# GpSimd instead of VectorE scales the queries, and three of SP's transfers change place, in a fused attention and FFN kernel

## The chip, the cores and the metric

The kernel runs on one core of a Trainium2 chip. The metric is the time of one execution on the device, in microseconds (us). Several runs of a kernel give a median. One more execution is recorded by the hardware profiler, and all rows below come from it.

The engines are called as the profile calls them: PE is TensorE (the matrix unit; PEld is its weight load), DVE is VectorE, ACT is ScalarE, POOL is GpSimd, and SP is SyncE, which here issues all transfers in one order of its own (SPq in the rows).

## What is computed

Windowed attention over q, k, v of shape 4 x 8 x 768 x 64 (batch, heads, positions, head width), then a feed-forward net (FFN) with a rational function in its middle, over the 3072 tokens:

```python
scores = q @ k.T / sqrt(D) - slope[h] * dist          # dist: distance, or n_local for a global key
keep   = (key < n_global) | ((0 <= rel) & (rel < n_local))    # n_global = 8, n_local = 96
a      = softmax(where(keep, scores, -1e9))
x      = (a @ v), heads side by side                  # 3072 x 512
h      = x @ w_in                                     # 3072 x 2048
P      = a0 + a1*h + a2*h**2 + a3*h**3
Q      = 1 + |b0|*|h| + |b1|*h**2
out    = (P / (Q + 1e-6)) @ w_out                     # 3072 x 512
```

## The kernel before, in words

**Tiles and units.** A unit u is two heads on one tile of 128 positions. There are 96 units, four to a tile and eight to a chunk of 256 tokens, so 12 chunks. A chunk has eight FFN parts f, each 256 of the 2048 inner columns; there are 96 parts too. From unit 24 on, units are handled as pairs (u even, u and u+1: four heads).

**Steps.** The main loop of `windowed` counts steps t. Step t issues the work of several stages, each for its own unit or part: FFN part k = t - 12 goes through its first product (`st_ffn1`, L340), the part before it finishes its function, and the part two back goes through its second product (`st_ffn2`, L434). The attention of the pairs runs ahead in the same loop: even steps start a pair's loads, odd steps start its scores. The second product of part f thus stands two steps behind its first on PE, and in between lie, for one part: ACT's three operations on h (L365 to L367), the sum of two of them (`st_sum`, L379, on POOL for nearly all parts), ACT's logarithm and exponential (L390, L391), three operations of DVE (L395 to L397), ACT's rounded copy g (L405) and its remainder (`st_low`, L408, on POOL for nearly all parts). PE needs both copies for the second product.

**A pair of units.** For pair u the stages are: `st_load` (L179, L180: q and k into a tile nat, two buffers); `st_split`, which scales q by a factor per head (L497, DVE) and transposes the scaled q and the k in blocks of 32 (L500, DVE) into sp; `st_scatter` (L508, four transfers from sp to a block of DRAM, zq); `st_gather` (L515, back from zq into qk); `st_score` (L590, PE); the maximum, the exponentials, the sum and the norm (L625 on DVE, L634 on ACT, L639 and L641 on DVE, L647 on POOL); `st_pT` (L667, DVE's transpose into T); `st_spread` (L678, four transfers from T to z in DRAM); `st_pTE` (L694, back as pT, two buffers); and `st_pv` (L713, PE: four units at once, the product with the values). The values come as vt (`load_v`, L187: the pair's own tile of positions) and vp (`load_vp`, L198 and L199: the tile before it, six and two buffers). A chunk's output goes from the accumulator into a tile o (L467, ACT in the paired stage) and out by `st_send` (L474).

**What sets the order.** The first part of the program (the list LEAD, up to about unit 30) has the order of every engine written out by hand. After it, PE and SP issue in the order in which the loop writes the stages; each stage has a priority within its step (the table PRI). ACT, DVE and POOL get their order from a scheduler, which may place an instruction ahead of its step if it holds it to be ready. On the chip each engine then runs its instructions strictly in that order, and an instruction that waits holds up all behind it. SP does the same with its transfers.

**Where the loop puts the edits.** In the loop, `on(name, u, kinds)` writes the stages `kinds` of unit u at step t: before the change, odd steps write sr (gather) for t+1, tw (spread) for t-3 and zw (scatter) for t+3; even steps write P (pT) for t-4, L (q and k) for t+6, V (vt) for t and vp for t-4; the split for t+4 is written ahead of the FFN's function, and T for t-2 near the end of the even step. The last part of a chunk writes O and D (the output's copy and its transfer) in its own, odd, step.

Of the kernel before, what the change touches and what calls it, by code (L numbers as in the profile page):

```python
# [2 lines left out]

# [6 lines left out]
F32 = mybir.dt.float32  # L10
# [4 lines left out]
ALU = mybir.AluOpType  # L15
PSUM = bass.MemoryType.PSUM

P = 128
# [16 lines left out]
FIXED = 30  # L35
# [8 lines left out]
SUM_V = ((0, 1), (1, 1), (2, 1), (0, 2), (1, 2), (2, 2), (1, 3), (0, 5), (0, 6), (1, 7))  # L44
# [98 lines left out]
def tile_kernel(ctx: ExitStack, tc: tile.TileContext, q, k, v, n_global, n_local,  # L143
                w_in, w_out, ca, cb, out):
    nc = tc.nc
# [6 lines left out]
    NCH = B * S // TOK  # L152
# [30 lines left out]
    def load_v(u):  # L183
        c, t, p, b, i = unit(u)
        hs = slice(2 * p, 2 * p + 4)
        vts[u // 2] = vt = pl.ldp.tile([P, 4, D], F32, tag="vt", name=f"vt{u}", bufs=6)
        nc.sync.dma_start(out=vt, in_=v[b, hs, i * P:(i + 1) * P, :].rearrange("h s d -> s h d"))  # L187


# [2 lines left out]
    def load_vp(u):  # L192
        c, t, p, b, i = unit(u)
        if u < PAIRS or i == 0:
            return
        hs = slice(2 * p, 2 * p + 4)
        vps[u // 2] = vp = pl.ldp.tile([P, 4, D], F32, tag="vp", name=f"vp{u}", bufs=2)
        nc.sync.dma_start(out=vp[0:P - KB], in_=v[b, hs, (i - 1) * P + KB:i * P, :].rearrange("h s d -> s h d"))  # L198
        nc.sync.dma_start(out=vp[P - KB:], in_=v[b, hs, 0:KB, :].rearrange("h s d -> s h d"))  # L199

# [142 lines left out]


    BOTH = slice(0, 2)

    def side(f, early, late=False):
        if pl.split:
            return nc.gpsimd
        return nc.vector if f == NU - 2 or late or divmod(f, FPC) in early else nc.gpsimd  # L350
# [25 lines left out]

    def st_sum(f, ys=BOTH):
        a, s = (ew[f][n][:, ys] for n in "as")
        side(f, SUM_V).tensor_tensor(out=a, in0=a, in1=s, op=ALU.add)  # L379

    def st_ew2(f, ys=BOTH):
        st_poly(f, ys)
# [22 lines left out]
        nc.scalar.copy(out=gs[f][:, 0, ys], in_=ew[f]["u"][:, ys])  # L405

    def st_low(f, ys=BOTH):
        side(f, G_V, f == NU - 1 and ys == 1).tensor_tensor(out=gs[f][:, 1, ys], in0=ew[f]["u"][:, ys], in1=gs[f][:, 0, ys], op=ALU.subtract)  # L408

    def st_split_g(f, ys=BOTH):  # L410
        if not plain(f):
# [80 lines left out]
    def st_split(u):  # L492
        c, t, p, b, i = unit(u)
        if u < PAIRS or u % 2:
            return
        n = nat[u // 2]
        nc.vector.tensor_tensor(out=n[:, 0], in0=n[:, 0], in1=qsc[:, 2 * p:2 * p + 4].unsqueeze(2).broadcast_to([P, 4, D]),  # L497
                                op=ALU.mult)
        sp[u] = s = pl.att.tile([P, 4, 4, KB], F32, tag="rawq", name=f"sp{u}", bufs=2)
        nc.vector.transpose(out=s.rearrange("p b z t -> p z b t"),  # L500
                            in_=n.rearrange("p z (y x) (c d) -> p (z y) (x c) d", x=2, d=KB))
# [254 lines left out]
    def windowed():  # L756
# [26 lines left out]
        def part(kind, *args):  # L783
            if (kind, *args) not in done:
                done.add((kind, *args))
                parts[kind](*args)
# [20 lines left out]
        lead = [(c, j) for z in range(2) for c in range(2) for j in range(z * HALF, HALF if z == 0 else FPC)]  # L807
        steps = [c * FPC + j for c, j in lead] + list(range(2 * FPC, NU))

        for t in range(NU + LAG + F2):  # L810
            k = t - LAG
            u0 = t - 3 - run_of(t - 4)

            def on(name, u, *kinds):
                if 0 <= u < NU:
                    tc.cur_priority = base + 1000 * t + PRI[name]
                    for kind in kinds:
                        part(kind, u)

            def ffn(name, k, kind, *args):  # L820
                if 0 <= k < NU:
                    tc.cur_priority = base + 1000 * t + PRI[name]
                    part(kind, steps[k], *args)

            def ffn2(name, k, x):
                if 0 <= k < NU:
                    c, j = divmod(steps[k], FPC)
                    tc.cur_priority = base + 1000 * t + PRI[name]
                    part("f2", steps[k], x)
                    if j == cut_of(c) - 1 and j < FPC - 1:  # L830
                        part("H", c, x)
                    if j == FPC - 1:
                        part("O", c, x)
                        part("D", c, x)

            if k == NU - 2:
                with tc.manual_schedule(engines={mybir.EngineType.Activation, mybir.EngineType.DVE, mybir.EngineType.Pool, mybir.EngineType.SP}):
# [2 lines left out]
                        token(word, True)  # L840
                break
            fixed = t >= FIXED
            if t % 2:
                on("gather", t + 1, "sr")
                on("load", t - 3, "tw")
                on("load", t + 3, "zw")
            else:
                on("load", t - 4, "P")
                on("load", t + 6, "L")
                on("load", t, "V")  # L850
                on("load", t - 4, "vp")
            if t < FIXED:
                on("score", t - 2, "s", "kg", "t")
                on("soft", t - 2, "x", "r")
# [7 lines left out]
            if t < FIXED:  # L862
# [2 lines left out]
                    on("pv", u0, "o", "vg")  # L865
                    on("x", u0, "y", "z")
                on("qkE", t, "qE", "kG")
            if t % 2 == 0:
                on("split", t + 4, "sp")
                on("split", t - 2, "kG")  # L870
            ffn("ew3", k - 1, "e3")
            if t < FIXED:
                on("norm", t - 2, "n")
# [5 lines left out]
                ffn("ew4", k - 1, "gl")  # L879
            ffn("ew2", k, "e2")  # L880
            ffn("ew2", k, "eq")
            if fixed:
                on("score", t - 1, "t")
                for u in (t - 1, t) if t % 2 else (t - 1,):
                    on("soft", u, "x", "r")
                    on("norm", u, "n")
            on("pT", t - 2, "T")
            if t < FIXED:
                on("pT", t - 3, "P")
            ffn2("ffn2a", k - F2, 0)  # L890
# [167 lines left out]
```

## Time and profile before

| what | value |
|---|---|
| median of 3 runs | 748.62 us (747.9 to 755.06) |
| the profiled execution | 753.98 us, of which 752.2 us is the span from first to last instruction |
| mean granted clock of PE | 0.967 of full speed |
| busy share of the span | PE 92%, DVE 74%, ACT 71%, POOL 46% |

PE has the highest share, but the average hides the stages: the first 230 us load and convert the weights and run the written-out order, the stretch from 230 to 690 us is the paired stage at its steady pace, and the rest is the FFN's tail. A row of a timeline gives the start, the length, the engine, the line, the operation and its tiles; in square brackets stands how long the engine had been idle before it and which instruction ended that. "x4" are four instructions merged into a row. [...]

### The profile page before, as it was taken

To read this page: it belongs to the slowest core of one execution; us is meant where nothing else is said; L and a number is where in the kernel's file an instruction comes from. 1 tells how busy PE (TensorE), PEld (TensorE's weight loads), DVE (VectorE), ACT (ScalarE), POOL (GpSimd) and SP (SyncE) were. 2 spreads that over 40 slices of the span, in tenths; PEclk is the share of its full clock that TensorE was granted. 3 is DMA by queue.
4 is the path that set the end of the run, shared out by engine and by line. 5 is a ranking of instruction groups with operands and counts; after the bars stand their busy time and mean duration, and the time that the engine had idled before them with its cause. 6 is when DMAs were issued, how large, how long until landed. Compare 5 with 4: busy or idle time off the path is not lost.

```text
span 752.2 us, 17016 instructions
## 1 busy us (share of the span) xinstructions
PE 689.7 (92%) x6167; PEld 587.1 (78%) x6167; DVE 558.2 (74%) x1355; ACT 531.4 (71%) x1174; POOL 343.8 (46%) x451
## 2 busy tenths in 40 slices
PE   5799998999489998989997998998996989999996
PEld 4576777677478887878886887887885978989995
DVE  5899998989657767778667777767775767665665
ACT  6899996967257757757775766766765757766764
POOL 2354558464225435445434444454443534544441
PEclk9999999999798999999999999999998999999999
DMA  8874536031673483483364483383264483250001
GB/s 201 239 219 145 151 120 207 13 99 38 164 189 103 118 215 103 115 217 78 112 178 108 117 217 97 111 223 76 87 161 104 109 214 102 83 164 2 28 1 34
DMA packets 161212, 95.20 MB, mean 127 GB/s; under 512 B 100064, under 2 KB 141152, under 8 KB 161120
## 3 DMA queue, kind: packets, MB, share of 16 engines
q1 hardware_dynamic: 161120, 94.02, 46.9%
q8 instruction: 51, 0.84, 0.5%
q14 instruction: 41, 0.34, 0.1%
HBM read 66.39 MB, written 27.59 MB: 125 GB/s over the span
## 4 chain that ended last, share of the span: by engine, by line
PE 54%; ACT 13%; DMA 9%; DVE 8%; SPq 8%; issue 4%; POOL 4%; DVEq 0%; POOLq 0%
PE h L340 22%; PE acc L434 22%; PE o L713 4%; ACT pr L634 3%; PE s L590 3%; DMA vp<-in_v_dram 2%; DMA z<-T 2%; DMA nat<-in_k_dram 2%; ACT fu L365 2%; SPq L678 1%; ACT fa L366 1%; POOL g L408 1%; DVE q L396 1%; POOL pr L647 1%; POOL fa L379 1%
## 5 line engine op out<-in xcount | busy, mean ns | idle before, releaser
L379 POOL TENSOR_TENSOR fa<-fa,fs 128x512 f32<-128x512 f32 (+1 forms) x86 | 110.0, 1279 | 173.7 <-ACT fs L367 164.6
L647 POOL TENSOR_SCALAR pr<-pr,stats 128x160 f32<-128x160 f32 (+2 forms) x170 | 68.5, 420 | 163.1 <-DVE stats L641 118.7
L434 PE MATMUL acc<-h,g 128*128 128x512 f32 x336 | 117.2, 411 | 16.1 <-POOL g L408 11.6
L390 ACT ACTIVATE fs<-fa,coef 128x512 f32<-128x512 f32 (+1 forms) x97 | 69.9, 720 | 77.6 <-POOL fa L379 74.7
L434 PE MATMUL acc<-wout_h,g 128*128 128x512 f32 x352 | 118.9, 398 | 3.2 <-ACT g L405 2.0
L408 POOL TENSOR_TENSOR g<-fu,g 128x512 fp32r<-128x512 f32 x84 | 108.6, 1293 | 19.9 <-ACT g L405 10.8
L395 DVE SCALAR_TENSOR_TENSOR fu<-fu,coef,q 128x512 f32<-128x512 f32 (+1 forms) x97 | 71.7, 739 | 45.4 <-ACT q L391 43.7
L365 ACT ACTIVATE fu<-h,coef 128x512 f32<-128x512 f32 x94 | 72.9, 776 | 45.7 <-PE h L340 45.0
L634 ACT ACTIVATE pr<-pr,stats 128x160 f32<-128x160 f32 (+2 forms) x192 | 82.3, 431 | 32.2 <-DVE stats L625 32.0
L340 PE MATMUL h<-xh,win_h 128*128 128x256 f32 x352 | 102.9, 292 | 0.1
L340 PE MATMUL h<-xh,h 128*128 128x256 f32 x352 | 101.7, 289 | 0.0
L340 PE MATMUL h<-xl,win_h 128*128 128x256 f32 x352 | 99.5, 283 | 0.5 <-DVE xl L752 0.5
L340 PE MATMUL h<-xl,h 128*128 128x256 f32 x352 | 98.8, 281 | 0.0
L374 DVE TENSOR_TENSOR fu<-fu,h 128x512 f32<-128x512 f32 (+1 forms) x97 | 65.3, 673 | 35.2 <-ACT fs L367 35.2
L434 PEld LDWEIGHTS acc<-h,g 128*128 128x128 f32 x336 | 66.2, 199 | 31.6 <-POOL g L408 13.9
L434 PEld LDWEIGHTS acc<-wout_h,g 128*128 128x128 f32 x352 | 66.9, 191 | 16.7 <-POOL g L408 2.2
L405 ACT CAST g<-fu 128x512 fp32r<-128x512 f32 (+1 forms) x88 | 54.5, 619 | 33.5 <-DVE fu L397 33.3
L375 DVE SCALAR_TENSOR_TENSOR fu<-fu,coef,h 128x512 f32<-128x512 f32 (+1 forms) x97 | 71.2, 734 | 2.5
L396 DVE SCALAR_TENSOR_TENSOR q<-fa,coef,q 128x512 f32<-128x512 f32 (+1 forms) x97 | 72.2, 744 | 0.0
L340 PEld LDWEIGHTS h<-xh,win_h 128*128 128x128 f32 x352 | 67.3, 191 | 4.8 <-issue 2.3
L340 PEld LDWEIGHTS h<-xh,h 128*128 128x128 f32 x352 | 66.6, 189 | 4.3 <-issue 2.8
L340 PEld LDWEIGHTS h<-xl,win_h 128*128 128x128 f32 x352 | 67.4, 192 | 2.1 <-DVE xl L752 0.7
(262 smaller groups left out, 1709.7 us busy)
## 6 DMA issues: line engine op xcount, KB each, us to landing
pT<-z SPq DMA_DIRECT2D x30, 512.0 KB, 3.9
z<-T SPq DMA_DIRECT2D x120, 80.0 KB, 2.2
zq<-sp SPq DMA_DIRECT2D x144, 64.0 KB, 1.8
qk<-zq SPq DMA_DIRECT2D x36, 256.0 KB, 3.2
r<-in_moe_w_in_dram SPq DMA_DIRECT2D x16, 512.0 KB, 5.2
r<-in_moe_w_out_dram SPq DMA_DIRECT2D x16, 512.0 KB, 3.8
nat<-in_q_dram SPq DMA_DIRECT2D x48, 128.0 KB, 4.2
nat<-in_k_dram SPq DMA_DIRECT2D x48, 128.0 KB, 4.2
```

The source lines that it names most:

```text
L340: nc.tensor.matmul(out=h_of(f, y), lhsT=w[:, fs], rhs=x[:, ct, :], start=(n == 0), stop=(n == 3 * NCT - 1))
L365: nc.scalar.activation(out=u, in_=h, func=AF.Identity, scale=a3, bias=a2)
L374: nc.vector.tensor_tensor(out=u, in0=u, in1=h, op=ALU.mult)
L375: nc.vector.scalar_tensor_tensor(out=u, in0=u, scalar=a1, in1=h, op0=ALU.add, op1=ALU.mult)
L379: side(f, SUM_V).tensor_tensor(out=a, in0=a, in1=s, op=ALU.add)
L390: nc.scalar.activation(out=s, in_=a, func=AF.Ln, bias=q1)
L395: nc.vector.scalar_tensor_tensor(out=u, in0=u, scalar=a0, in1=r, op0=ALU.add, op1=ALU.mult)
L396: nc.vector.scalar_tensor_tensor(out=r, in0=a, scalar=q1, in1=r, op0=ALU.add, op1=ALU.mult)
L408: side(f, G_V, f == NU - 1 and ys == 1).tensor_tensor(out=gs[f][:, 1, ys], in0=ew[f]["u"][:, ys], in1=gs[f][:, 0, ys], op=ALU.subtract)
L434: nc.tensor.matmul(out=acc, lhsT=gs[f][:, z, y, ts], rhs=w, start=(start and n == 0), stop=(stop and n == 2))
L634: nc.scalar.activation(out=d, in_=d, func=AF.Exp, scale=-1.0, bias=st[:, x:x + 1], accum_out=st[:, 2 + 2 * x:3 + 2 * x])
L647: (nc.vector if u < NORMS else nc.gpsimd).tensor_scalar(out=d, in0=d, scalar1=st[:, 6 + x:7 + x], scalar2=0.0, op0=ALU.mult, op1=ALU.add)
```

## The change

Four edits. The scaling of q moves from DVE to POOL. In the paired stage, the split (scaling, transpose and a small copy) is written later in its step, behind the FFN's sums, and its instructions are issued only behind the last of POOL's FFN operations (sum or remainder) recorded up to there. vp is loaded two steps earlier, and shares eight buffers with vt. In SP's order the spread of T follows directly on T, ahead of the gather; pT is written at the end of the odd step; and a chunk's output goes out one step later, behind the spread.

```diff
     def load_v(u):
-        vts[u // 2] = vt = pl.ldp.tile([P, 4, D], F32, tag="vt", name=f"vt{u}", bufs=6)
+        vts[u // 2] = vt = pl.ldp.tile([P, 4, D], F32, tag="vt", name=f"vt{u}", bufs=8)
...
     def load_vp(u):
-        vps[u // 2] = vp = pl.ldp.tile([P, 4, D], F32, tag="vp", name=f"vp{u}", bufs=2)
+        vps[u // 2] = vp = pl.ldp.tile([P, 4, D], F32, tag="vt", name=f"vp{u}", bufs=8)
...
+    paced = {}
+
+    def pace(i):
+        paced[i.ins.engine] = i.ins
+
+    def behind(engine):
+        return tc.issue_after(paced[engine]) if paced.get("on") else nullcontext()
...
     def st_sum(f, ys=BOTH):
-        side(f, SUM_V).tensor_tensor(out=a, in0=a, in1=s, op=ALU.add)
+        pace(side(f, SUM_V).tensor_tensor(out=a, in0=a, in1=s, op=ALU.add))
...
     def st_low(f, ys=BOTH):
-        side(f, G_V, f == NU - 1 and ys == 1).tensor_tensor(out=gs[f][:, 1, ys], in0=ew[f]["u"][:, ys], in1=gs[f][:, 0, ys], op=ALU.subtract)
+        pace(side(f, G_V, f == NU - 1 and ys == 1).tensor_tensor(out=gs[f][:, 1, ys], in0=ew[f]["u"][:, ys], in1=gs[f][:, 0, ys],
+                                                                 op=ALU.subtract))
...
     def st_split(u):
-        nc.vector.tensor_tensor(out=n[:, 0], in0=n[:, 0], in1=qsc[:, 2 * p:2 * p + 4].unsqueeze(2).broadcast_to([P, 4, D]),
+        nc.gpsimd.tensor_tensor(out=n[:, 0], in0=n[:, 0], in1=qsc[:, 2 * p:2 * p + 4].unsqueeze(2).broadcast_to([P, 4, D]),
                                 op=ALU.mult)
...
                     if j == FPC - 1:
                         part("O", c, x)
-                        part("D", c, x)
+                        if c < NCH - 1:
+                            late.append((c, x))
+                        else:
+                            part("D", c, x)
...
             fixed = t >= FIXED
+            paced["on"] = t >= FIXED
             if t % 2:
                 on("gather", t + 1, "sr")
-                on("load", t - 3, "tw")
                 on("load", t + 3, "zw")
+                on("load", t - 3, "P")
             else:
-                on("load", t - 4, "P")
                 on("load", t + 6, "L")
                 on("load", t, "V")
-                on("load", t - 4, "vp")
+                on("load", t - 2, "vp")
...
-            if t % 2 == 0:
-                on("split", t + 4, "sp")
-                on("split", t - 2, "kG")
             ffn("ew3", k - 1, "e3")
...
             ffn("ew2", k, "eq")
+            if t % 2 == 0:
+                with behind(mybir.EngineType.Pool):
+                    on("split", t + 4, "sp")
+                    on("split", t - 2, "kG")
...
-            on("pT", t - 2, "T")
+            on("pT", t - 2, "T", "tw")
+            for c, x in late:
+                on_send(c, x)
+            late.clear()
```

What this does to the order of the instructions shows best in the program itself. In the names, the number behind a tile's letters is its unit or FFN part (nat52 is the q and k of pair 52, fu34 belongs to part 34); the number behind the underscore is of no account.

DVE, in the paired stage, before: the stretch from the transpose of pair 44's probabilities (T44) to the maximum of pair 46's scores.

```order
L667 STREAM_TRANSPOSE T44_3851<-pr44_3717 128x4x5x32
L375 SCALAR_TENSOR_TENSOR fu33_3750<-fu33_3750,coef_60,h33_3722 128x512
L395 SCALAR_TENSOR_TENSOR fu33_3750<-fu33_3750,coef_60,q33_3821 128x512
L396 SCALAR_TENSOR_TENSOR q33_3821<-fa33_3751,coef_60,q33_3821 128x512
L397 SCALAR_TENSOR_TENSOR fu33_3750<-q33_3821,fu33_3750 128x512
L374 TENSOR_TENSOR fu34_3836<-fu34_3836,h34_3805 128x512
L497 TENSOR_TENSOR nat52_3797<-nat52_3797,qsc_67 128x256
L375 SCALAR_TENSOR_TENSOR fu34_3836<-fu34_3836,coef_60,h34_3805 128x512
L500 STREAM_TRANSPOSE sp52_4023<-nat52_3797 128x4x4x32
L625 ISA pr46_3906,stats_59<-s46_0_3876,near_74 128x160
```

The same stretch of DVE with the change:

```order
L675 STREAM_TRANSPOSE T44_3852<-pr44_3722 128x4x5x32
L382 SCALAR_TENSOR_TENSOR fu33_3755<-fu33_3755,coef_60,h33_3727 128x512
L402 SCALAR_TENSOR_TENSOR fu33_3755<-fu33_3755,coef_60,q33_3819 128x512
L403 SCALAR_TENSOR_TENSOR q33_3819<-fa33_3756,coef_60,q33_3819 128x512
L404 SCALAR_TENSOR_TENSOR fu33_3755<-q33_3819,fu33_3755 128x512
L381 TENSOR_TENSOR fu34_3834<-fu34_3834,h34_3806 128x512
L382 SCALAR_TENSOR_TENSOR fu34_3834<-fu34_3834,coef_60,h34_3806 128x512
L508 STREAM_TRANSPOSE sp50_3850<-nat50_3613 128x4x4x32
L633 ISA pr46_3911,stats_59<-s46_0_3881,near_74 128x160
```

The scaling is gone from DVE, and the transpose at this place is that of pair 50 and no longer that of pair 52.

SP, the same place, before: from the outputs of chunk 3 (o3) on.

```order
L474 DMA out_0_dram<-o3_0_3783 128x512
L474 DMA out_0_dram<-o3_1_3792 128x512
L694 DMA pT42_3795<-z1_86 128x2x512
L179 DMA nat52_3797<-in_q_dram 128x4x64
L180 DMA nat52_3797<-in_k_dram 128x4x64
L187 DMA vt46_3800<-in_v_dram 128x4x64
L198 DMA vp42_3802<-in_v_dram 96x4x64
L199 DMA vp42_3802<-in_v_dram 32x4x64
L515 DMA qk_64<-zq0_87 128x512
L678 DMA z0_85<-T44_3851 32x5x128 x4
L508 DMA zq1_88<-sp50_3819 32x4x128 x4
L694 DMA pT44_3999<-z0_85 128x2x512
```

And SP with the change:

```order
L179 DMA nat52_3798<-in_q_dram 128x4x64
L180 DMA nat52_3798<-in_k_dram 128x4x64
L187 DMA vt46_3801<-in_v_dram 128x4x64
L198 DMA vp44_3803<-in_v_dram 96x4x64
L199 DMA vp44_3803<-in_v_dram 32x4x64
L686 DMA z0_85<-T44_3852 32x5x128 x4
L482 DMA out_0_dram<-o3_0_3788 128x512
L482 DMA out_0_dram<-o3_1_3796 128x512
L523 DMA qk_64<-zq0_87 128x512
L516 DMA zq1_88<-sp50_3850 32x4x128 x4
L702 DMA pT44_3879<-z0_85 128x2x512
L179 DMA nat54_4004<-in_q_dram 128x4x64
```

The outputs stand behind the loads and the spread of T44 instead of ahead of them, the gather into qk stands behind that spread, and the vp loaded beside nat52 is that of pair 44 instead of pair 42. The load of nat52 itself has not moved against T44.

POOL, before, in the paired stage around the norm of pair 62 (pr62) and the FFN parts 49 to 52 (fa: sum, g: remainder):

```order
L408 TENSOR_TENSOR g49_5353<-fu49_5258,g49_5353 128x512
L647 TENSOR_SCALAR pr62_5414<-pr62_5414,stats_59 128x160 x4
L408 TENSOR_TENSOR g50_5477<-fu50_5344,g50_5477 128x512
L379 TENSOR_TENSOR fa51_5469<-fa51_5469,fs51_5470 128x512
L379 TENSOR_TENSOR fa52_5549<-fa52_5549,fs52_5550 128x512
L408 TENSOR_TENSOR g51_5557<-fu51_5468,g51_5557 128x512
L647 TENSOR_SCALAR pr64_5616<-pr64_5616,stats_59 128x160 x4
```

POOL with the change, the same stretch:

```order
L505 TENSOR_TENSOR nat66_5121<-nat66_5121,qsc_67 128x256
L415 TENSOR_TENSOR g49_5351<-fu49_5263,g49_5351 128x512
L655 TENSOR_SCALAR pr62_5419<-pr62_5419,stats_59 128x160 x4
L415 TENSOR_TENSOR g50_5482<-fu50_5342,g50_5482 128x512
L386 TENSOR_TENSOR fa51_5474<-fa51_5474,fs51_5475 128x512
L386 TENSOR_TENSOR fa52_5549<-fa52_5549,fs52_5550 128x512
L505 TENSOR_TENSOR nat68_5306<-nat68_5306,qsc_67 128x256
L415 TENSOR_TENSOR g51_5557<-fu51_5473,g51_5557 128x512
L655 TENSOR_SCALAR pr64_5621<-pr64_5621,stats_59 128x160 x4
```

One scaling per pair now stands on POOL, between a sum and a remainder. In the written-out first part it stands where the list has the pair's split: for pair 24, POOL has it directly behind the clearing of the tile qk,

```order
L547 COPY near_74<-qk_64 32x128
L548 MEMSET qk_64 128x2560
L505 TENSOR_TENSOR nat24_1278<-nat24_1278,qsc_67 128x256
L263 TENSOR_SCALAR w0_12f_1448<-r0_12_1294 128x512
L290 TENSOR_TENSOR w0_6l_1458<-w0_6f_1013,wout_h_63 128x512
```

while DVE's transpose of pair 24 keeps its place, where before the scaling stood right ahead of it on the same engine.

## Rows read from the trace of the kernel before

**Rows 1.** Stretches: start:end, length, busy time (count) by engine, granted clock, DMA share, GB/s.

```profile
230.00:690.00 460.00, 435.28 (x4492) 382.66 (x4492) 330.33 (x800) 316.41 (x673) 215.36 (x260) 0.97 0.51 131
690.00:742.00 52.00, 52.00 (x334) 47.45 (x335) 35.34 (x54) 36.64 (x64) 21.36 (x18) 1.00 0.03 11
```

**Rows 2.** What PE waited for, 230 to 690 us: total, times, longest.

```profile
PE acc L434 <- POOL g L408: 11.6, 5, 2.8
PE o L713 <- DMA vp<-in_v_dram: 7.4, 6, 2.0
PE acc L434 <- ACT g L405: 4.5, 2, 2.9
PE o L713 <- DMA vt<-in_v_dram: 0.9, 1, 0.9
```

**Rows 3.** Timelines of PE and DVE around the wait at 516 us.

```profile
516.53 0.74 PE L434 MATMUL acc<-h,g 128*128 128x512 f32 x2 [2.06 <-POOL g L408]
...
507.27 0.42 DVE L497 TENSOR_TENSOR nat<-nat,qsc 128x256 f32<-128x256 f32 x1 [2.21 <-DMA nat<-in_q_dram]
```

**Rows 4.** Timeline of SP's transfers, 484 to 504 us.

```profile
484.11 0.84 SPq L474 DMA_DIRECT2D out_dram<-o  x2
...
487.74 1.41 SPq L199 DMA_DIRECT2D vp<-in_v_dram  x1
...
503.21 0.47 SPq L179 DMA_DIRECT2D nat<-in_q_dram  x1
```

**Rows 5.** What DVE and SP waited for, 230 to 690 us: total, times, longest.

```profile
DVE nat L497 <- DMA nat<-in_q_dram: 41.5, 24, 4.3
...
SPq L474 <- ACT o L467: 70.7, 8, 11.7
```

**Rows 6.** Timeline of PE around 491 us.

```profile
491.82 0.44 PE L713 MATMUL o<-pT,vp 128*64 128x128 f32 x4 [1.20 <-DMA vp<-in_v_dram]
```

**Rows 7.** A stretch, as rows 1: four microseconds behind a wait of PE.

```profile
459.20:463.30 4.10, 4.06 (x10) 2.77 (x10) 3.45 (x5) 3.33 (x6) 2.02 (x2) 0.58 0.44 105
```

**Rows 8.** Operations of one line, 230 to 690 us: ns min/median/max, first and last start.

```profile
L497 DVE TENSOR_TENSOR nat<-nat,qsc x27: 414/427/1507, 242.7 to 616.5; 128x256 f32<-128x256 f32 x27
...
L379 POOL TENSOR_TENSOR fa<-fa,fs x66: 1264/1288/1478, 229.7 to 687.3; 128x512 f32<-128x512 f32 x66
```

**Rows 9.** Timelines of DVE and POOL around 490 us.

```profile
488.80 0.69 DVE L374 TENSOR_TENSOR fu<-fu,h 128x512 f32<-128x512 f32 x1 [0.34 <-ACT fs L367]
...
491.65 0.28 DVE L625 CUSTOM_DVE_ANT_0 pr<-s,near 128x160 f32<-128x160 f32 x1
...
488.79 1.28 POOL L379 TENSOR_TENSOR fa<-fa,fs 128x512 f32<-128x512 f32 x1 [2.65 <-ACT fs L367]
```

**Rows 10.** Timelines of POOL and PE, 257 to 259 us, without a wait of PE.

```profile
257.32 1.29 POOL L408 TENSOR_TENSOR g<-fu,g 128x512 fp32r<-128x512 f32 x1
...
258.99 0.39 PE L434 MATMUL acc<-wout_h,g 128*128 128x512 f32 x1
```

**Rows 11.** Timelines of POOL and DVE in the written-out part, 115 to 191 us.

```profile
117.88 2.24 POOL L540 MEMSET qk<- 128x2560 f32 x1
...
115.84 0.71 DVE L500 STREAM_TRANSPOSE sp<-nat 128x512 f32<-128x512 f32 x1
...
120.94 1.75 DVE L282 SCALAR_TENSOR_TENSOR w_12f<-w_12f,r 128x512 int32<-128x512 int32 x1 [1.13 <-POOL w_12f L263]
...
166.67 0.42 DVE L497 TENSOR_TENSOR nat<-nat,qsc 128x256 f32<-128x256 f32 x1 [1.89 <-DMA nat<-in_q_dram]
...
189.98 0.87 POOL L647 TENSOR_SCALAR pr<-pr,stats 128x160 f32<-128x160 f32 x2 [1.78 <-DVE stats L641]
...
190.24 0.71 DVE L500 STREAM_TRANSPOSE sp<-nat 128x512 f32<-128x512 f32 x1
```

**Rows 12.** PE at the start of the paired stage: a row of its timeline, and a stretch.

```profile
223.60 0.50 PE L434 MATMUL acc<-wout_h,g 128*128 128x512 f32 x1 [1.96 <-ACT g L405]
...
223.50:229.50 6.00, 5.21 (x13) 3.86 (x14) 5.19 (x19) 5.36 (x15) 2.61 (x5) 0.57 0.02 6
```

More of the change, by code (lines that the diff above doesn't have):

```diff
@@ L1 @@
-from contextlib import ExitStack
+from contextlib import ExitStack, nullcontext
 from types import SimpleNamespace
@@ L808, in windowed @@
         steps = [c * FPC + j for c, j in lead] + list(range(2 * FPC, NU))
+        late = []
         for t in range(NU + LAG + F2):
@@ L833, in ffn2, with on_send @@
                         part("O", c, x)
-                        part("D", c, x)
+                        if c < NCH - 1:
+                            late.append((c, x))
+                        else:
+                            part("D", c, x)
+            def on_send(c, x):
+                tc.cur_priority = base + 1000 * t + PRI["load"]
+                part("D", c, x)
             if k == NU - 2:
```

## Prediction

> **What bounds the kernel now.** I read the stretches first. In the paired stage, 230 to 690 us, PE is busy 435.28 of 460 us at a granted clock of 0.97; in the tail behind it, 52.00 of 52 us at 1.00 [rows 1]. So PE is the engine to look at, and the paired stage loses time in two ways: PE stands still for 460 - 435.28 = 24.7 us, and its work is stretched by the clock. Next I asked what PE waited for there [rows 2]. Four rows hold 11.6 + 7.4 + 4.5 + 0.9 = 24.4 of those 24.7 us: the copies g of an FFN part, from POOL or ACT (16.1 us, seven waits), and the values, vp and once vt (8.3 us, seven waits). The clock goes with these waits. Behind the one that ends about 459 us it is 0.58 [rows 7], while the tail, where PE does not wait at all, has 1.00 [rows 1].
>
> The third view is the timeline around one wait on g, taken backwards. PE waits 2.06 us for POOL's remainder at 516.53; nine microseconds earlier DVE waited 2.21 us for nat, with the FFN's operations queued behind that scaling [rows 3]. The fourth, SP's timeline, tells why nat was late: its load was issued at 503.21, only four microseconds before DVE could go on at 507.27 [rows 3, 4]. SP issues in order, and its longest waits are the sends of the outputs, which wait for ACT's copy o: 70.7 us in eight waits. DVE's own largest wait is the consequence: 41.5 us for nat, 24 times, with one pair in 14.4 us ((616.5 - 242.7) / 26, first and last start of the scalings) [rows 5, 8]. The values suffer in the same queue. SP stood at a send until 484.11, issued vp at 487.74, and PE waited for it until 491.82 [rows 4, 6].
>
> **The change, part by part.** The sum is made on the profiled execution, 753.98 us (span 752.2).
>
> *vp, vt and the outputs in SP's order.* vp is issued one pair, 14.4 us, earlier; today it misses PE by 2.0 us at most [rows 2]. The sends stand behind the loads, and behind the spread of T, which is written a step later than the output's copy; I expect nothing of importance to stand behind a waiting send. The gather into qk moves behind the spread and can lose the time that SP waits for T; its reader is a step away, some 7 us (half of 14.4). So the waits on vp and vt go: **-8.3 us** (between -4, if half only change their cause, and -8.3).
>
> *The scaling behind POOL's FFN operations.* The order shows what matters: DVE's transpose behind T44 is now that of pair 50, where it was pair 52, while SP's load of nat52 kept its place against T44. The load has one pair, 14.4 us, more before anybody asks for it; the longest wait on it today is 4.3 us [rows 5]. A wait of DVE on nat can no longer arise at that place, and the waits on g that I followed come from there. Not all seven were followed, but all belong to the same chain of DVE, ACT and POOL. I take all: **-16.1 us** (between -8, half of them, and -16.1).
>
> *The clock.* Without the waits there is no ground for a lower clock than in the tail: (1.00 - 0.97) x 435.28 = **-13.1 us** (between half, -6.5, and -13.1). Half goes with half of the waits.
>
> *The price on POOL.* DVE's scaling takes 427 ns for 256 elements a partition. POOL's sum of 512 takes 1288 ns; half is 0.65 us [rows 8]. The trace shows no scaling on POOL, so the bounds are 0.43, DVE's own, and 1.29, the whole sum; I take 0.65, as POOL's operations here go by size. It stands between a sum and a remainder. The sum about 490 us ends at 488.79 + 1.28 = 490.07 [rows 9]; with 0.65 the scaling ends at 490.72, DVE's transpose (0.71 us [rows 11]) at 491.43, ahead of the maximum that starts at 491.65 today [rows 9]. So there DVE loses nothing. POOL has room: 316.41 of 460 us busy; 27 scalings add 17.6. Where the remainder is next and its part is short of time, the margin is small: at 257.32 + 1.29 = 258.61 it ends 0.38 us ahead of the first product that stands at 258.99 [rows 10]. That product is of the other copy, so not every late remainder holds it. I take **+1.5 us** (0 to +5).
>
> [...] The row gives 0.65 / 0.427 = 1.5 times DVE's duration. [...]
>
> *The start of the paired stage.* PE waits 1.96 us at 223.60 for ACT's g, and has a clock of 0.57 in the six microseconds there: 5.21 x 0.43 = 2.2 us [rows 12]. It is the same chain, with the new order already in force: **-4.2 us** (0 to -4.2).
>
> *The written-out part.* Here DVE's order stands, and its transpose of pair 24 now waits for a scaling that POOL does behind clearing qk: 117.88 + 2.24 + 0.65 = 120.8 instead of 115.84, so +5.0 [rows 11]. DVE's wait of 1.13 us on w_12f at 120.94 is swallowed: -1.1. The wait of 1.89 us for nat at 166.67, and the scaling's 0.42, leave DVE: -2.3. The transpose at 190.24 comes behind POOL's pr (189.98 + 0.87) and a scaling: 191.5, so +1.3 [rows 11]. Together **+2.9 us** (-2, if DVE has slack there, to +6.3, if nothing is swallowed).
>
> Sum: -8.3 - 16.1 - 13.1 + 1.5 - 4.2 + 2.9 = -37.3; 753.98 - 37.3 = 716.7 us. The profiled execution is 5.4 us above the median of the runs, 748.62, and I take that off: **711 us**.
>
> **The rivals.**
>
> *A new wait in every cycle.* POOL's remainder comes 0.65 to 1.3 us later once a pair, against a margin of 0.4, and DVE's maxima stand behind a transpose that waits for POOL. For it: the margin above, and that DVE is busy 382.66 of 460 us [rows 1], with no room to catch up. Against it: DVE gets 27 x 0.43 = 11.5 us of work less. Price: half of the 32 steps of two (460 / 14.4) give PE a wait of 0.5 us, 8 us, and half of the clock's 13.1 stays, 6.5: 711 + 14.5 = about **726 us**.
>
> *Half of the waits stay.* SP's sends were the cause of the late loads, but other things hold SP too (T, which it now waits for ahead of three more transfers). Then half of 8.3, 16.1 and 13.1 remain: 711 + 18.8 = about **730 us**.
>
> *It does nothing.* The waits on g move from one cause to another of the same length, and the clock stays: 749 less nothing, about **748 us**. For it: 74% of DVE and 71% of ACT are near to PE's share, so something else could be due at the same time. Against: the tail runs at 1.00 without a wait [rows 1].
>
> *Slower: POOL waits in DVE's stead.* If nat still came late, the 41.5 us in 24 waits (1.73 us each) would pass to POOL's scaling, and right behind it stands a remainder with 0.4 us to spare: 24 x 1.33 = 32 us of waits at PE where there are 16.1 now, and the clock low for six microseconds behind each of them as behind the one at 223.60, 24 x 2.2 = 53 where there are 13.1. It decides from 0.4 us of lateness on. 749 - 8.3 + 15.9 + 39.9 = about **796 us**; were half of them hidden, 772. Against it stands the pair by which the load is now ahead.
>
> **How the numbers follow.** Forecast 0.62; a new wait in every cycle 0.14; half of the waits stay 0.11; nothing 0.06; slower 0.07. The forecast's own range by its bounds is 705 to 722 us: the lower end takes the written-out part at -2 and POOL at 0, the upper one the written-out part at +6.3, POOL at +5 and the start at 0. The range over all goes up to 732, which takes in the second and third case; what lies above is 0.13, and below 703 some 0.05. Faster by over 1% (below 741 us): 0.62 + 0.14 + 0.11 = 0.87. Within 1%, about what a measurement can tell from no change: 0.06. Slower: 0.07.
>
> **What would show it.** Right: DVE has no waits on nat, POOL's scalings take about 0.65 us and wait for no transfer; PE's rows for vp are gone and those for g below 3 us; the clock of the paired stage is 0.99 or more, and it lasts about 426 us instead of 460. In the written-out part DVE's transpose of pair 24 waits some 5 us for POOL. Wrong: waits of POOL's scaling on nat, a maximum or a remainder that follows them late, a wait of PE for g every 14 us, or SP's order held by T with qk or pT late in its stead.

## The result and the profile after

The changed kernel takes 712.93 us (median of 4 runs, 712.47 to 714.27), against 751.84 us (747.9 to 755.38, 4 runs) for the kernel before: a ratio of 0.949, 95% interval 0.942 to 0.955. 711 us was forecast, with a range of 703 to 732. The profiled execution takes 712.47 us, with a span of 710.7.

The stretches, after; the columns are those of [rows 1]. The last row is cut so that it begins and ends with the same matmuls of the FFN's first product as the row of the kernel before under it (the 385th and the 1825th of L340's 2112).

```profile
230.00:650.00 420.00, 420.00 (x4495) 374.11 (x4494) 316.88 (x777) 317.04 (x673) 228.60 (x288) 1.00 0.58 145
241.70:629.10 387.40, 387.40 (x4194) 344.83 (x4193) 294.04 (x734) 294.48 (x631) 213.48 (x273) 1.00 0.60 150
```

```profile
244.10:671.20 427.10, 402.38 (x4193) 353.11 (x4192) 308.71 (x760) 293.99 (x631) 198.98 (x245) 0.97 0.52 135
```

PE now works for every microsecond of the paired stage, at a granted clock of 1.00, as it did only in the tail before [rows 1]. For the same work, 427.10 us became 387.40. Of the 39.7 us, 427.10 - 402.38 = 24.7 are waits that are gone; 402.38 - 387.40 = 15.0 are busy time that is gone, most of it by the clock (an estimate from these rows: (1.00 - 0.97) x 402.38 = 12 us).

What PE waited for between 190 us and the end of the stage is in two rows; neither lies in the paired stage. The first is a wait at the border between the written-out part and the loop, which has nothing to do with g or the values. The kernel before has it too, 1.2 us shorter (last row, of that kernel); the prediction did not look at it.

```profile
PE s L598 <- DMA qk<-zq: 10.5, 1, 10.5
PE o L721 <- PE s L598: 0.5, 1, 0.5
```

```profile
PE s L590 <- DMA qk<-zq: 9.3, 1, 9.3
```

The scalings on POOL, 230 to 690 us: line, engine, tiles, count, busy us, mean ns, idle time before them; it answers to [rows 8].

```profile
L505 POOL TENSOR_TENSOR nat<-nat,qsc 128x256 f32<-128x256 f32 x29 | 17.7, 611 | 0.0
```

No scaling waits for its load. DVE waits for POOL instead, briefly (the stage's waits, answering to [rows 5]):

```profile
DVE sp L508 <- POOL nat L505: 11.1, 25, 0.5
```

### The profile page after: what moved, and what is told of

Read it like the earlier page. It is cut to its first block, busy times and chain, and to the rows that moved or that the text cites. A ratio compares the mean times of both kernels' runs of the same rounds, so it can differ in the third digit from the quotient of the medians.

```text
span 710.7 us, 17118 instructions
## 1 busy us (share of the span) xinstructions
PE 671.8 (95%) x6167; PEld 576.8 (81%) x6167; DVE 537.8 (76%) x1319; ACT 532.3 (75%) x1174; POOL 361.9 (51%) x487
## 4 chain that ended last, share of the span: by engine, by line
PE 79%; ACT 11%; DVE 3%; issue 2%; SPq 2%; DMA 1%; POOL 1%; POOLq 0%; ACTq 0%
PE h L340 33%; PE acc L442 30%; PE o L721 6%; PE s L598 4%; PE acc L438 2%; PE h L332 2%; ACT pr L642 2%; ACT r L271 1%; ACT fu L372 1%; DMA r<-in_moe_w_in_dram 1%; ACT qzero L561 1%; PE s L584 1%; ACT fs L397 1%; ACT fa L373 1%; ACT q L398 1%
## 5 line engine op out<-in xcount | busy, mean ns | idle before, releaser
L442 PE MATMUL acc<-wout_h,g 128*128 128x512 f32 x352 | 117.1, 393 | 0.7 <-POOL g L415 0.7
L415 POOL TENSOR_TENSOR g<-fu,g 128x512 fp32r<-128x512 f32 x84 | 107.9, 1285 | 15.4 <-ACT g L412 11.5
L442 PE MATMUL acc<-h,g 128*128 128x512 f32 x336 | 110.7, 391 | 0.0
L340 PE MATMUL h<-xh,win_h 128*128 128x256 f32 x352 | 101.8, 289 | 0.2 <-DVE fu L382 0.2
L340 PE MATMUL h<-xh,h 128*128 128x256 f32 x352 | 101.2, 287 | 0.0
L340 PE MATMUL h<-xl,win_h 128*128 128x256 f32 x352 | 98.7, 280 | 0.6 <-DVE xl L760 0.6
L340 PE MATMUL h<-xl,h 128*128 128x256 f32 x352 | 98.4, 280 | 0.0
L442 PEld LDWEIGHTS acc<-h,g 128*128 128x128 f32 x336 | 63.1, 188 | 11.9 <-issue 0.2
L340 PEld LDWEIGHTS h<-xh,win_h 128*128 128x128 f32 x352 | 66.4, 189 | 4.6 <-issue 1.9
L340 PEld LDWEIGHTS h<-xh,h 128*128 128x128 f32 x352 | 66.2, 188 | 4.2 <-issue 2.8
L340 PEld LDWEIGHTS h<-xl,win_h 128*128 128x128 f32 x352 | 66.5, 189 | 2.1 <-DVE xl L760 0.8
L404 DVE SCALAR_TENSOR_TENSOR fu<-q,fu 128x512 f32<-128x512 f32 (+1 forms) x97 | 66.3, 683 | 2.2
```

Of the source, the lines that this page charges most:

```text
L340: nc.tensor.matmul(out=h_of(f, y), lhsT=w[:, fs], rhs=x[:, ct, :], start=(n == 0), stop=(n == 3 * NCT - 1))
L404: nc.vector.scalar_tensor_tensor(out=u, in0=r, scalar=2.0, in1=u, op0=ALU.subtract, op1=ALU.mult, reverse0=True)
L415: pace(side(f, G_V, f == NU - 1 and ys == 1).tensor_tensor(out=gs[f][:, 1, ys], in0=ew[f]["u"][:, ys], in1=gs[f][:, 0, ys], op=ALU.subtract))
L442: nc.tensor.matmul(out=acc, lhsT=gs[f][:, z, y, ts], rhs=w, start=(start and n == 0), stop=(stop and n == 2))
```

## The experiments

Before them I held one theory, A: the scaling is held back, so its load has a pair more time, and that is most of the gain; vp is the rest. Its rivals were B, that the outputs ahead of the loads in SP's queue were the cause, and C, that relief of DVE is what counts. The first four kernels and the fifth split the change into its three parts: the engine of the scaling, its place, and SP's order.

**SP's new order alone.**

The kernel before, with these lines of the change and the list `late` for the outputs, and vt and vp in eight shared buffers:

```diff
-                on("load", t - 3, "tw")
                 on("load", t + 3, "zw")
+                on("load", t - 3, "P")
...
-                on("load", t - 4, "P")
...
-                on("load", t - 4, "vp")
+                on("load", t - 2, "vp")
...
-            on("pT", t - 2, "T")
+            on("pT", t - 2, "T", "tw")
+            for c, x in late:
+                on_send(c, x)
+            late.clear()
```

> The kernel before with the change's order of SP alone (vp a pair earlier, eight shared buffers, spread right behind T, pT late, outputs a step later); the scaling stays on VectorE where the scheduler put it. Theory A (what counts is that the scaling is held back, so that its load is a pair ahead): only the waits on vp and vt go, 8.3 us, and their share of the clock's loss, about 4.5, so about 739 us (731 to 745), with VectorE's waits for nat still above 25 us. Theory B (the outputs ahead of the loads in SP's queue were the cause): about 717 us (713 to 725), VectorE's waits for nat under 10 us.

Measured: 770.84 us (767.01 to 776.34), against 746.3 beside it; ratio 1.031 (1.023 to 1.040). Slower by 3%, which no theory had. The waits of that kernel, 230 to 690 us:

```profile
DVE nat L497 <- DMA nat<-in_q_dram: 55.6, 26, 4.4
...
PE acc L434 <- POOL g L408: 25.2, 13, 2.8
...
PE acc L434 <- ACT o L467: 5.3, 5, 1.6
```

No send holds SP there any more, the waits on vp are gone, and yet DVE's waits for nat have grown from 41.5 to 55.6 us [rows 5] and PE's for POOL's g from 11.6 to 25.2 [rows 2]. The order of DVE tells why. Counted over the 27 pairs from 42 on: in the kernel before, the scheduler placed the scaling of pair u behind T of pair u - 8 (12 times) or u - 10 (15 times); with SP's new order it is u - 10 all 27 times. What that costs can be read in the kernel before: the 15 scalings behind u - 10 waited 30.2 us for nat, 2.0 us each, the 12 behind u - 8 only 11.3, 0.9 each. 27 waits of 2.0 us are 54, near the 55.6 measured. The load that the scaling of pair u needs is issued only behind the transfers of T of pair u - 10, so the further ahead the scaling stands, the longer DVE waits. One turn, DVE and SP:

```profile
485.45 0.85 DVE L497 TENSOR_TENSOR nat<-nat,qsc 128x256 f32<-128x256 f32 x1 [1.74 <-DMA nat<-in_q_dram]
486.22 0.83 DVE L667 STREAM_TRANSPOSE T<-pr 128x640 f32<-128x640 f32 x1
```

```profile
487.08 1.78 SPq L678 DMA_DIRECT2D z<-T  x4
488.90 0.45 SPq L515 DMA_DIRECT2D qk<-zq  x1
489.39 1.91 SPq L508 DMA_DIRECT2D zq<-sp  x4
491.47 0.38 SPq L694 DMA_DIRECT2D pT<-z  x1
491.89 0.49 SPq L179 DMA_DIRECT2D nat<-in_q_dram  x1
```

T stands behind a scaling that waits for its load, and the next load stands behind that T's spread: a ring. B falls.

**The scaling on POOL behind the FFN's operations, SP's old order.**

The changed kernel with the lines above undone, the buffers of vt and vp too, as in:

```diff
-                on("load", t - 2, "vp")
+                on("load", t - 4, "vp")
...
-            on("pT", t - 2, "T", "tw")
+            on("pT", t - 2, "T")
```

> The changed kernel with SP's old order (vp, spread, pT and outputs where they were): the scaling on GpSimd behind the FFN's operations alone. Theory A: the waits on g go, those on vp stay; 713 + 8.3 + about 4.5 = 726 us (719 to 732). Theory B: the loads are late behind the outputs as before; about 738 us (732 to 748).

Measured: 725.72 us (724.95 to 726.18); ratio 0.970 (0.964 to 0.976). As A had it, to the microsecond. PE's waits of the stage are those on vp, as before (and one short wait), and the seven on g are gone:

```profile
PE o L721 <- DMA vp<-in_v_dram: 8.6, 6, 2.4
PE o L721 <- DVE stats L633: 0.5, 1, 0.5
```

**Without the hold-back.**

```diff
-            paced["on"] = t >= FIXED
+            paced["on"] = False
```

> The changed kernel without the rule that GpSimd's scaling is issued behind the FFN's operations: the scheduler puts it and VectorE's transpose a pair earlier. Theory A: the waits for nat are back, now on GpSimd ahead of a sum or a remainder, some 20 of them of 1 to 2 us; 740 us or more, by the rival of the prediction up to 796. Theory B: the order of SP suffices; 713 to 717 us.

Measured: 727.01 us (726.27 to 727.4); ratio 0.972 (0.966 to 0.978). Between the two theories: DVE's transposes stand at u - 8 or u - 10 again, and the waits for nat are back, on POOL; but they are 12 and not 24, and in the stage PE feels little of them. Nearly half of what this kernel loses lies ahead of that: from the 289th to the 385th matmul of L340 it takes 32.3 us where the changed kernel takes 26.0; POOL stands 6.30 us for nat at 225.65, and PE 3.3 us for g.

```profile
POOL nat L505 <- DMA nat<-in_q_dram: 11.9, 12, 2.0
...
PE acc L442 <- POOL g L415: 3.8, 7, 1.1
```

**The scaling held back, but on DVE.** The hold-back is on DVE's own FFN operation, so the transposes stand at u - 6 as in the changed kernel; apart from the engine, only the operation that holds the scaling back differs.

```diff
-        nc.vector.scalar_tensor_tensor(out=u, in0=u, scalar=a1, in1=h, op0=ALU.add, op1=ALU.mult)
+        pace(nc.vector.scalar_tensor_tensor(out=u, in0=u, scalar=a1, in1=h, op0=ALU.add, op1=ALU.mult))
...
-        nc.gpsimd.tensor_tensor(out=n[:, 0], in0=n[:, 0], in1=qsc[:, 2 * p:2 * p + 4].unsqueeze(2).broadcast_to([P, 4, D]),
+        nc.vector.tensor_tensor(out=n[:, 0], in0=n[:, 0], in1=qsc[:, 2 * p:2 * p + 4].unsqueeze(2).broadcast_to([P, 4, D]),
                                 op=ALU.mult)
...
-                with behind(mybir.EngineType.Pool):
+                with behind(mybir.EngineType.DVE):
```

> The changed kernel with the scaling back on VectorE, in the whole program, but held back there behind the FFN's operation of the step as the change does on GpSimd. Theory A (the place counts, not the engine): 708 to 714 us; the 3.6 us lost in the written-out part come back, 27 x 0.43 = 11.5 us more on VectorE are hidden. Theory C (relief of VectorE counts): 720 to 726 us, with waits of TensorE for g.

Measured: 728.62 us (728.56 to 729.09); ratio 0.974 (0.968 to 0.980). C holds here, and by more than its own sum. Time is lost in waits for g, and the scaling has tripled, from a median of 427 ns [rows 8] to 1347. How much is due to the 0.43 us that it takes alone, and how much to the rest, was not separated (waits of PE; then the scalings of 230 to 690 us: count, ns min/median/max, first and last start).

```profile
PE acc L442 <- POOL g L415: 13.0, 16, 1.2
```

```profile
L505 DVE TENSOR_TENSOR nat<-nat,qsc x29: 1270/1347/1462, 233.0 to 612.8; 128x256 f32<-128x256 f32 x29
```

**Held back on DVE, with SP's old order.** The kernel above with SP's edits undone.

```diff
-                on("load", t - 2, "vp")
+                on("load", t - 4, "vp")
...
-            on("pT", t - 2, "T", "tw")
+            on("pT", t - 2, "T")
```

> The kernel before with one thing new: the split is written behind the FFN's sums and held back behind VectorE's FFN operation, so that VectorE scales and transposes one to two pairs later than before; engine and SP's order as before. If hold-back, relief of VectorE and SP's order simply add up: the 728.6 us of the kernel with SP's new order and the scaling held on VectorE, plus the 12.8 us by which SP's old order was slower on GpSimd, 741 us (736 to 746), without waits of VectorE for nat. If the hold-back were nearly all of the gain: 725 to 732 us. If it were worth nothing without the relief: 748 to 755 us.

Measured: 737.85 us (737.41 to 738.27); ratio 0.981 (0.975 to 0.986). The hold-back alone is worth some 15 us (1.4 to 2.5%). Once it is there, SP's edits give 8.5 us with the scaling on DVE and 12.8 with it on POOL, by the spans of the profiled executions. DVE does not wait for nat, but the scaling is as long as in the run above. Its place on DVE, and what POOL does at that time:

```profile
481.42 0.75 DVE L382 SCALAR_TENSOR_TENSOR fu<-fu,coef,h 128x512 f32<-128x512 f32 x1
482.08 1.32 DVE L505 TENSOR_TENSOR nat<-nat,qsc 128x256 f32<-128x256 f32 x1
...
481.85 1.28 POOL L415 TENSOR_TENSOR g<-fu,g 128x512 fp32r<-128x512 f32 x1
```

DVE's scaling begins 0.23 us into POOL's remainder and ends 0.27 us after it. So it is with all 29, here and in the run above: each begins in a remainder of POOL, within 0.3 us of its start, and ends some 0.28 us after it.

The three parts together, in us (the changed kernel ran twice). The entries from 725.7 to 728.6 and that of 770.8 come from one chip, the others from others, and the kernel before beside them took 746.3 to 752.7; a few microseconds between entries of different chips say little.

| scaling | SP's old order | SP's new order |
|---|---|---|
| DVE, where the scheduler puts it | 746.3 to 752.7 | 770.8 |
| DVE, held back | 737.9 | 728.6 |
| POOL, where the scheduler puts it | not run | 727.0 |
| POOL, held back | 725.7 | 712.9, 714.5 |

**POOL's margin: the scaling twice.**

```diff
         nc.gpsimd.tensor_tensor(out=n[:, 0], in0=n[:, 0], in1=qsc[:, 2 * p:2 * p + 4].unsqueeze(2).broadcast_to([P, 4, D]),
                                 op=ALU.mult)
+        nc.gpsimd.tensor_tensor(out=n[:, 0], in0=n[:, 0], in1=qsc[:, 2 * p:2 * p + 4].unsqueeze(2).broadcast_to([P, 4, D]),
+                                op=ALU.mult)
```

This kernel computes something else: its scores carry the factor twice.

> The changed kernel with the scaling done twice on GpSimd (q is multiplied by its factor twice, so the scores are scaled twice): 0.61 us more a pair between a sum and a remainder. GpSimd has room: 713 to 716 us (about 1 us of it in the written-out part), no waits of TensorE for g. The margin of 0.4 us decides: half of 32 steps wait 0.2 to 0.6 us, 719 to 726 us, with waits of TensorE for g from GpSimd.

Measured: 719.01 us (717.72 to 720.8); ratio 0.956 (0.950 to 0.962). The time is that of the margin's theory, the place is not. PE waits 0.8 us for g, and is busy 419.11 of 420 us between 230 and 650; the wait at the border has grown from 10.5 to 13.4 us. At the 385th matmul of L340 the kernel is already 3.6 us behind the changed one, and 6.4 at the end (in four executions with the changed kernel's written-out part, that matmul starts at 240.0 to 241.7 us). So in the paired stage 0.61 us more a pair costs under 3 us in all, and a written-out scaling on POOL costs more than it seemed.

```profile
PE s L600 <- DMA qk<-zq: 13.4, 1, 13.4
PE acc L442 <- POOL g L415: 0.8, 2, 0.4
```

**SP's edits one by one.** The changed kernel with vp back in its old place,

```diff
-                on("load", t - 2, "vp")
+                on("load", t - 4, "vp")
```

and, in another kernel, with the outputs back in theirs, so that none is put off:

```diff
-                        if c < NCH - 1:
+                        if c < 0:
```

> The changed kernel with vp loaded where it was (two steps later), all else of SP's order new. If vp is what SP's order gives: TensorE's waits on vp are back, 6 to 9 us, and the time is 720 to 726 us, as with all of SP's old order (725.7). If it is the outputs and the spread: 713 to 716 us.

> The changed kernel with the outputs sent in their old place (their own odd step, ahead of the next loads), all else new. If vp is what SP's order gives: 713 to 715 us. If a send that holds SP for up to 11.7 us is what made transfers late: 717 to 726 us, with waits of TensorE on vp or qk behind the sends.

Measured: 714.99 us (710.84 to 716.86) with vp back, 713.75 us (711.03 to 714.86) with the outputs back; the ratios, 0.951 (0.946 to 0.957) and 0.949 (0.944 to 0.955), are the changed kernel's. Neither has a wait of PE on vp. So neither of the two edits is needed where the other stands: vp a pair earlier can bear the sends, and without the sends ahead of it vp is in time at its old place. Both have the new places of the spread and of pT; whether these alone would do was not tried. With the outputs back, SP stands at the sends for 26.1 us up to the last loads, against 70.7 in the kernel before [rows 5], and PE feels none of it (SP's waits, 230 to 630 us):

```profile
SPq L516 <- DVE stats L633: 110.0, 29, 6.4
SPq L482 <- ACT o L475: 26.1, 8, 9.2
```

**The written-out part.** The changed kernel once more, and three variants of its first part on the same chip. One has the scaling on DVE in the written-out part,

```diff
-        nc.gpsimd.tensor_tensor(out=n[:, 0], in0=n[:, 0], in1=qsc[:, 2 * p:2 * p + 4].unsqueeze(2).broadcast_to([P, 4, D]),
+        (nc.gpsimd if paced.get("on") else nc.vector).tensor_tensor(out=n[:, 0], in0=n[:, 0], in1=qsc[:, 2 * p:2 * p + 4].unsqueeze(2).broadcast_to([P, 4, D]),
```

one has pair 30's split, scatter and gather early in the list LEAD,

```diff
-... n27 kG26 t28 x28 ...
+... n27 kG26 t28 sp30 zw30 sr30 x28 ...
...
-r28 n28 sp30 zw30 D1_0 T26 ...
+r28 n28 D1_0 T26 ...
```

and one has both.

> The changed kernel once more, as it is, on the same chip as the three variants of the written-out part beside it: 711 to 715 us.

> The changed kernel with the scaling back on VectorE in the written-out part alone (pairs 24 to 32). The prediction's term for that part (+2.9 us) says it gives 2 to 3.5 us back: 710 us (709 to 712) where the changed kernel has 713. The runs with the scaling on VectorE throughout stood 1.5 us better than the changed kernel after sixteen FFN parts, by which it would be 711.5. If VectorE has slack there: no difference.

> The changed kernel with one more edit in the written-out order: pair 30's scaling, transpose, scatter and gather stand behind the maxima of pair 28 and no longer behind two more norms, a spread, two outputs and five loads in SP's order. TensorE's wait of 10.5 us for the gather at the border of the written-out part goes, and the slow clock of the ten us behind it (about 2.3 us): 700 to 703 us if nothing else is late there; 704 to 709 if the copies g of the FFN parts before it are late next; 711 or more if the wait only changes its cause.

> Both edits of the written-out part: scaling on VectorE there, and pair 30's transfers early. The two gains add: 1.5 to 3 us below the kernel with the early transfers alone; no gain over it if that kernel's remaining waits in the written-out part are not behind VectorE's transposes.

| kernel | median us | runs | ratio to before |
|---|---|---|---|
| changed, again | 714.54 | 711.51 to 716.12 | 0.953 (0.950 to 0.956) |
| DVE in the written-out part | 709.89 | 707.61 to 710.86 | 0.946 (0.943 to 0.949) |
| early transfers of pair 30 | 709.10 | 707.95 to 710.71 | 0.946 (0.943 to 0.949) |
| both | 708.26 | 705.89 to 708.83 | 0.944 (0.941 to 0.947) |

The first gains 4.6 us by the medians, more than the 2 to 3.5 that were expected; of it, the two profiled executions show 1.8 us up to the 385th matmul of L340, about what that stretch varies by, and no difference in pace from there to the end of the stage. Of the second, up to 14 were expected and 5.4 came, for the wait at the border has for the most part only changed its name: PE stands 7.6 us ahead of the product with the values of pairs 24 and 26. SP issues pT of pair 26 there at 200.44, behind the loads; PE goes on at 203.35.

```profile
203.35 1.97 PE L721 MATMUL o<-pT,vt 128*64 128x128 f32 x16 [7.58 <-issue]
...
200.44 0.36 SPq L702 DMA_DIRECT2D pT<-z  x1
```

Both together are the fastest kernel here, though over either alone they gain no more than these runs can tell; the gains don't add.

## Why the prediction was right, and where it was not

The time by stretches, cut at the same matmuls of L340 in both profiled executions (the 289th starts at 212.2 us before and 215.7 after):

| stretch | before | after | difference | forecast |
|---|---|---|---|---|
| to the 289th matmul | 212.2 | 215.7 | +3.5 | +2.9 |
| to the 385th | 31.9 | 26.0 | -5.9 | -4.2 |
| to the 1825th | 427.1 | 387.4 | -39.7 | -36.0 |
| to the end of the span | 81.0 | 81.6 | +0.6 | 0 |
| sum | 752.2 | 710.7 | -41.5 | -37.3 |

The number is nearer than the sum. The sum said 716.7 us for the profiled execution, which took 712.47, 4.2 less. The 5.4 us that were then taken off, because the profiled execution of the kernel before lies above its median, are not there in the changed kernel, whose own lies 0.5 us below its median. The two errors nearly cancel; that 711 meets 712.93 so closely is in part luck.

- *The waits on g, vp and vt (-16.1, -8.3).* Right in size: 24.7 us of waits are gone. That all seven waits on g are one chain of late scalings was argued from one of them; the kernel with the scaling held back on POOL and SP's old order has none of the seven, so all hung on the scaling.
- *The clock (-13.1).* Right in size: 15.0 us of busy time are gone. But not all of that is the clock, by the 12 us above. Held back on DVE, the scaling left PE busy for 392.79 us with the same stretch of matmuls at a clock of 1.00 (row below), 5.4 us more than 387.40; where these come from stays open. Nor did the clock go with every wait. In the kernel before it was 0.56 to 0.77 in the six us behind each of the seven waits on g, and 1.00 behind four of the six on vp.

```profile
240.20:646.00 405.80, 392.79 (x4193) 343.80 (x4193) 328.17 (x763) 293.89 (x632) 198.18 (x246) 1.00 0.57 144
```

- *The price on POOL (+1.5).* It was nothing in the stage. The scaling took 0.61 us (0.65 was estimated), and the kernel with two of them shows the room. The 0.612 us are 1.4 times the 0.427 that is DVE's median [rows 8]; 1.5 times was estimated.
- *The start of the stage (-4.2).* Right in mechanism, a little more in size: 5.9 us, and no wait of PE is left there.
- *The written-out part (+2.9).* Right in mechanism, and about right in size (+3.5; +2.3 in the other profiled execution of the changed kernel). DVE's transpose of pair 24 waits 5.30 us for the scaling that POOL does behind clearing qk:

```profile
120.33 0.61 POOL L505 TENSOR_TENSOR nat<-nat,qsc 128x256 f32<-128x256 f32 x1
...
120.97 0.71 DVE L508 STREAM_TRANSPOSE sp<-nat 128x512 f32<-128x512 f32 x1 [5.30 <-POOL nat L505]
```

Three steps behind these numbers failed.

First, "SP's timeline, tells why nat was late: ... its longest waits are the sends", and DVE's waits for nat as "the consequence". The sends were only the longest row. With the sends out of the way DVE waited more for nat, 55.6 us; with all of SP's old order and the scaling held back, no scaling waited for nat, on DVE or on POOL. What made nat late was the scheduler, which placed the scaling one to two pairs ahead of where the change has it, behind a T whose own transfers stand ahead of that load in SP's queue: 2.0 us of waiting for each scaling behind u - 10, 0.9 behind u - 8.

Second, SP's edits were given a term of their own, "-8.3". It holds only with the other edit. On the kernel before, they cost 24.5 us (770.8 against 746.3), because the scheduler then reordered DVE. With the scaling held back on POOL they are worth 12.8 us (723.5 - 710.7 of span). And the load of vp a pair earlier, with which the prediction's reason begins, is not needed for that: with it undone alone, no wait on vp came back.

Third, the engine. The move from DVE to POOL had no gain in the sum, and DVE's relief stood in the first rival as "27 x 0.43 = 11.5 us". In the kernel before the scalings of the stage take 17.4 us, not 11.5, since 11 of the 27 begin in a sum or a remainder of POOL that has 0.2 us or more to run, and take 518 to 1507 ns; the median hid it:

```profile
L497 DVE TENSOR_TENSOR nat<-nat,qsc 128x256 f32<-128x256 f32 x27 | 17.4, 644 | 41.6 <-DMA nat<-in_q_dram 41.5
```

Held back on DVE they take 29 x 1.35 = 39.2 us, and the kernel is some 15 us slower than with POOL. So the hold-back at this place could not have brought the forecast gain on DVE (a place on DVE clear of POOL's operations was not tried); that the forecast came out is owed to an engine change whose worth was put at nothing.

Of the rivals, the new wait in every cycle did not come: PE has no wait at all in the stage. "POOL waits in DVE's stead" was tried in the kernel without the hold-back: mechanism as described, price far too high. The waits in the stage were half as many, and PE stood there for 3.8 us where the rival had 32: 727 us, not 772 to 796. "Half of the waits stay" took SP's sends for the cause of the late loads; the kernel with SP's new order alone speaks against that, and PE has none of those waits left.

## What to carry to other kernels

Where a scheduler sets the order, count how many rounds ahead of its data it has placed an operation, before its wait is put down to the queue that brings the data; an edit to the queue alone can push the operation further ahead. Read the durations of one operation as a spread and not as a median: here a maximum of 1507 ns beside a median of 427 said that its place beside POOL's work had a price. And when a stage has become one engine's solid work, look for the rest elsewhere: here in the first 230 us.

## What the runs showed of the hardware

DVE's scaling, begun while a sum or a remainder ran on POOL, looked as if it made no headway beside it, and ended some 0.28 us after it. In the two runs held back on DVE it was so 29 times of 29: 1.35 us on average, where the median of the kernel before is 0.43. In the kernel before, the 11 named above, which began in a sum or a remainder with 0.2 us or more to run, all ended 0.27 to 0.29 us after it. FFN operations of DVE right beside it, as the one at 481.42 above, were not stretched: the 67 of that line took 737 ns on average in the run of that row, and in the kernel before none of the stage's 66 took more than 749 ns, though 47 of them began in a sum or a remainder of POOL with 0.3 us or more to run. What makes this difference no run shows.

It also went the other way round. In that stage of the kernel before, the six sums and remainders of POOL that began with 0.3 us or more of a scaling of DVE still to run took 1.46 to 1.55 us, where the median is 1.29; the three that began with less than 0.2 us of one left took 1.28 to 1.32. The longest of the six, beside a scaling that took its 0.43:

```profile
490.03 1.55 POOL L408 TENSOR_TENSOR g<-fu,g 128x512 fp32r<-128x512 f32 x1
...
490.02 0.43 DVE L497 TENSOR_TENSOR nat<-nat,qsc 128x256 f32<-128x256 f32 x1 [0.54 <-DMA nat<-in_q_dram]
```

The clock did not follow the length of a wait alone. In the run held back on DVE with SP's old order, a wait of 2.06 us on vp was followed by six us at a mean of 0.72, between two levels (of the 920 windows of half a microsecond from 230 to 690 us in the kernel before, 854 read 1.00 and 51 read 0.50), and a longer one, of 2.31 us, by six at 1.00:

```profile
318.11:324.11 6.00, 6.00 (x51) 5.67 (x52) 4.36 (x16) 2.96 (x10) 2.99 (x6) 0.72 0.85 214
593.29:599.29 6.00, 6.00 (x59) 5.58 (x60) 4.12 (x15) 4.04 (x13) 2.78 (x5) 1.00 0.74 197
```

In the kernel before, a wait of 1.28 us left it at 1.00, one of 1.98 us was followed by 0.72, and one of 1.26 us, with another of 0.93 us close ahead of it, by 0.72 too. The ten waits of 0.8 to 1.2 us in the run held back on DVE with SP's new order all left it at 1.00. What tells such waits apart stays open; for the sum it matters that the 13.0 us of short waits in that run cost no clock, though the stage was 18.4 us longer than the changed kernel's, 5.4 of them busy time, as said above.
